# Cosformer attention feeding a low-rank mixer and an MLP: first two batches staged by halves of the heads with a direct transposed mixer output, tails padded to full 128x128 matmuls

## The chip, the cores and the metric

The kernel runs on one core of a Trainium2 chip. The metric is device time in microseconds (us) of one execution; a run is repeated and the median is taken. Names of engines as in the profile: PE (TensorE, with PEld for its weight loads), DVE (VectorE), ACT (ScalarE), POOL (GpSimd), SP (SyncE, which here only issues DMAs).

## What is computed

Eight batches, eight heads, 576 positions, head size 64. Linear attention with cosine weights comes first, then a token mixer of rank 32, then an MLP over the channels (512 to 2048 to 512):

```python
def phi(x, c, s):
    r = np.maximum(x, 0.0)
    return np.concatenate([r * c, r * s], axis=-1)
q_p = phi(q, cos_w, sin_w); k_p = phi(k, cos_w, sin_w)
kv = np.einsum('bhsf,bhsd->bhfd', k_p, v)
z = np.sum(k_p, axis=2)
num = np.einsum('bhsf,bhfd->bhsd', q_p, kv)
den = np.einsum('bhsf,bhf->bhs', q_p, z)[..., None] + 1e-06
x = num / den                       # heads side by side: (8, 576, 512)
h = x.transpose(0, 2, 1) @ U @ V
u = x + h.transpose(0, 2, 1)
out = u + np.maximum(u @ w_ch1, 0.0) @ w_ch2
```

Inputs and output are float32; the kernel computes its matmuls in bfloat16 with float32 sums.

## The kernel before

The 576 positions of a batch are four chunks of 128 and a **tail** of 64. An even batch keeps its tail in partitions 0 to 63, an odd one in 64 to 127, so that the tails of a pair of batches share one tile in the MLP. `tail(b)` is that slice of rows, and every tail operation before the MLP runs on 64 rows alone: the tail's matmuls take 64 of the array's 128 rows (or columns), and the mixer's two matmuls take 32 (`U_bf` is 128x32, `V_bf` has 32 rows).

For one batch the front part, called the mixer here, is this chain:

- loads of k, v and q (SP), `k_prep` (L184, cos and sin half of relu(k), on DVE), `q_prep` (L182, the same for q, on ACT), `v_prep` (L176, L178, casts of v on POOL into `v_ext`, whose 65th column is one, so that the sum z comes out of the same matmul);
- `kv_unit` (L219): per head five accumulating matmuls, the fifth the tail; a unit is four heads, evicted by DVE (L226);
- `qtr_unit` (L238): per chunk eight transposes of q_p on PE, evicted into `q_pT` (L111);
- `x_unit` (L254): per chunk eight matmuls that give numerator and denominator side by side, then on DVE denominator plus 1e-6 (L263), reciprocal (L266), product (L269) into `x_bf`;
- `A_unit` (L281, L288): x against U over all five chunks; `u_unit` (L298, L301): per chunk V against that, plus x, into `u_bf`; `utr_unit` (L318): four transposes per chunk of u into `uT`, which the MLP reads.

The MLP works on a pair of batches in 72 slots: sixteen `g1_main` for each batch (L332, four matmuls of 512 columns, evicted with the relu by ACT at L339), four `g1_tail` (L350) and 36 `g2_part` (L375, four matmuls each; every fourth ends in a DVE add and an output DMA, L386, L389, L393).

All order is written out by hand: each engine runs its instructions in the order of the program. First comes the mixer of batch 0 (in two halves of the heads up to x, L444 to L457), then the sixteen `g1_main(0, j)`, then the whole mixer of batch 1, then the four pairs. In a pair, `pe_plan` and `prep_plan` give the mixer's pieces of the next two batches slot numbers, and they are put between the MLP's slots. `load(b + 1)` is put eight slots after the start of batch b's plan, all three tensors at once; `k_prep` of batch 4 stands at slot 58 of pair 0, and `load(4)` at slot 55. Buffers: `kst` two, `qst` and `vst` one each, so a load waits for the preparation of the batch before.

Of the kernel before, what the change touches and what calls it, by code (L numbers as in the profile page):

```python
# [17 lines left out]
def kernel(  # L18
# [14 lines left out]
    H = 8  # L33
# [128 lines left out]
    def cast_uv():
        nc.gpsimd.tensor_copy(out=U_bf, in_=stU)
        nc.gpsimd.tensor_copy(
            out=V_bf[:, 0:4, :], in_=stV[:, 0:512].rearrange("r (p c) -> r c p", c=4)
        )
        nc.gpsimd.tensor_copy(out=V_bf[:, 4, 0:TS], in_=stV[:, 512:S])


    k_p, q_p, q_pT, kv_sb, x_bf, x_tl, A_sb = {}, {}, {}, {}, {}, {}, {}  # L170
    u_bf, u_tl, uT, uT_tl = {}, {}, {}, {}

    def v_prep(b, h0=0, h1=H):
        vx = v_ext[b % 2]
        for c in range(4):
            nc.gpsimd.tensor_copy(out=vx[:, c, h0:h1, 0:D], in_=vst[b][:, h0:h1, c, :])  # L176
        if h0 == 0:
            nc.gpsimd.tensor_copy(out=vx[tail(b), 4, :, 0:D], in_=vt[b][tail(b)])  # L178
# [9 lines left out]
    def k_prep(b, c, eng, h0=0, h1=H, half=None):  # L188
        if b not in k_p:
            k_p[b] = pool.tile([P, 5, H, 2 * D], BF16, tag="k_p", bufs=1, name="k_p")  # L190
        rows = slice(0, P) if c < 4 else tail(b)
        src = kst[b][:, h0:h1, c, :] if c < 4 else kt[b][rows, h0:h1, :]
        for i, w in enumerate((cosw, sinw)):
            if half in (None, i):
                scaled_relu(
                    eng, k_p[b][rows, c, h0:h1, i * D : i * D + D], src, w[rows, c : c + 1]
                )

    def q_prep(b, c, eng, h0=0, h1=H, half=None):
        if (b, c) not in q_p:  # L200
            q_p[b, c] = pool.tile([P, H, 2 * D], BF16, tag="q_p", bufs=5, name="q_p")
        rows = slice(0, P) if c < 4 else tail(b)
        src = qst[b][:, h0:h1, c, :] if c < 4 else qt[b][rows, h0:h1, :]
        for i, w in enumerate((cosw, sinw)):
            if half in (None, i):
                scaled_relu(
                    eng, q_p[b, c][rows, h0:h1, i * D : i * D + D], src, w[rows, c : c + 1]
                )

    def kv_unit(b, hg, tag, bufs):  # L210
# [4 lines left out]
        for i in range(4):  # L215
            h = hg * 4 + i
            for c in range(5):
                rows = slice(0, P) if c < 4 else tail(b)
                nc.tensor.matmul(  # L219
                    out=acc[:, i, :],  # L220
                    lhsT=k_p[b][rows, c, h, :],
                    rhs=vx[rows, c, h, :],
                    start=(c == 0),
                    stop=(c == 4),
                )
        nc.vector.tensor_copy(out=kv_sb[b][:, hg * 4 : hg * 4 + 4, :], in_=acc)  # L226

    def cols(c):
        return slice(c * P, c * P + P) if c < 4 else slice(512, S)

    def qtr_unit(b, c, h0=0, h1=H, eng=None):
        if b not in q_pT:
            q_pT[b] = pool.tile([P, H, S], BF16, tag="q_pT", bufs=1, name="q_pT")
        n = P if c < 4 else TS
        rows = slice(0, P) if c < 4 else tail(b)
        t_ps = ps.tile([P, H, P], BF16, tag="T", bufs=1, name="t_ps")
        for h in range(h0, h1):
            nc.tensor.transpose(  # L238
                out=t_ps[:, h, 0:n], in_=q_p[b, c][rows, h, :], identity=ident[rows, rows]
            )  # L240
        cast(eng or nc.vector, q_pT[b][:, h0:h1, cols(c)], t_ps[:, h0:h1, 0:n])

    def x_unit(b, c, hgs, tag, bufs):
        if b not in x_bf:
            x_bf[b] = pool.tile([P, 4, DM], BF16, tag="x_bf", bufs=1, name="x_bf")
            x_tl[b] = pool.tile([P, DM], BF16, tag="x_tl", bufs=1, name="x_tl")
        n = P if c < 4 else TS
        rows = slice(0, P) if c < 4 else tail(b)
        ng = len(hgs)
        acc = ps.tile([P, ng, 512], FP32, tag=tag, bufs=bufs, name="x_ps")  # L250
        for g, hg in enumerate(hgs):
            for i in range(4):
                h = hg * 4 + i
                nc.tensor.matmul(  # L254
                    out=acc[rows, g, i * E : i * E + E],
                    lhsT=q_pT[b][:, h, cols(c)],
                    rhs=kv_sb[b][:, h, :],
# [8 lines left out]
        nc.vector.reciprocal(out=rec[rows], in_=rec[rows])  # L266
        dst = x_bf[b][:, c, :] if c < 4 else x_tl[b][rows, :]
        dst = dst[:, hgs[0] * 256 : hgs[0] * 256 + ng * 256]
        nc.vector.tensor_tensor(  # L269
            out=dst.rearrange("p (g i d) -> p g i d", g=ng, d=D),  # L270
            in0=view[:, :, :, 0:D],
            in1=rec[rows].unsqueeze(3).to_broadcast([n, ng, 4, D]),
# [3 lines left out]
    def A_unit(b, tag, bufs):  # L276
        A_sb[b] = pool.tile([R, DM], BF16, tag="A_sb", bufs=2, name="A_sb")
        a_ps = ps.tile([R, DM], FP32, tag=tag, bufs=bufs, name="a_ps")
        for c in range(5):
            rows = slice(0, P) if c < 4 else tail(b)  # L280
            nc.tensor.matmul(  # L281
                out=a_ps,
                lhsT=U_bf[rows, c, :],
                rhs=x_bf[b][:, c, :] if c < 4 else x_tl[b][rows, :],
# [3 lines left out]
        nc.vector.tensor_copy(out=A_sb[b], in_=a_ps)  # L288

    def u_unit(b, c, tag, bufs):  # L290
        if b not in u_bf:
# [4 lines left out]
        n = P if c < 4 else TS  # L296
        va = ps.tile([P, DM], FP32, tag=tag, bufs=bufs, name="va_ps")
        nc.tensor.matmul(  # L298
            out=va[rows, :], lhsT=V_bf[:, c, 0:n], rhs=A_sb[b], start=True, stop=True
        )  # L300
        nc.vector.tensor_tensor(  # L301
            out=u_bf[b][:, c, :] if c < 4 else u_tl[b // 2][rows, :],
            in0=x_bf[b][:, c, :] if c < 4 else x_tl[b][rows, :],
# [3 lines left out]

    def utr_unit(b, c, eng=None):
        if b not in uT:
            uT[b] = pool.tile([P, 4, 512], BF16, tag="uT", bufs=2, name="uT")  # L310
            if b % 2 == 0:
                uT_tl[b // 2] = pool.tile([P, 4, P], BF16, tag="uT_tl", bufs=2, name="uT_tl")
        rows = slice(0, P) if c < 4 else tail(b)
        n = P if c < 4 else TS
        t_ps = ps.tile([P, H, P], BF16, tag="T", bufs=1, name="t_ps")
        for d in range(4):
            src = u_bf[b][:, c, :] if c < 4 else u_tl[b // 2][rows, :]
            nc.tensor.transpose(  # L318
                out=t_ps[:, d, 0:n], in_=src[:, d * P : d * P + P], identity=ident[rows, rows]
            )  # L320
        dst = uT[b][:, :, cols(c)] if c < 4 else uT_tl[b // 2][:, :, rows]
        cast(eng or nc.vector, dst, t_ps[:, 0:4, 0:n])
# [4 lines left out]
    def g1_main(b, j):  # L327
# [3 lines left out]
        for d in range(4):  # L331
            nc.tensor.matmul(  # L332
                out=g_ps,
                lhsT=w1_bf[:, d, j * P : j * P + P],
                rhs=uT[b][:, d, :],
# [217 lines left out]
```

## Time and profile before

| what | value |
|---|---|
| median of 3 runs | 414.84 us (414.8 to 415.09) |
| the profiled execution's own time | 414.22 us |
| its span in the trace | 412.4 us |
| PE, DVE, ACT, POOL busy | 88%, 45%, 34%, 11% of the span |
| DMA queues busy | 38% of 16 engines' span |

The span runs from the first to the last instruction, so 1.8 us of the execution's own time lie around it. A busy PE in this page is not a PE at its peak: matmuls overlap, and a matmul of 512 columns is recorded with 383 to 388 ns while the next may start after 215. The time between starts is what counts, and the chain of waits shows it, since it holds each piece only once.

### The profile page before, as it was taken

The numbers are of one execution on the slowest core, as the hardware profiler recorded it, in microseconds if no ns is written. First come the engines' busy times: TensorE is split into PE (matmuls) and PEld (weight loads), VectorE is DVE, ScalarE is ACT, GpSimd is POOL, SyncE is SP. The second block draws the span as 40 slices with busy tenths as digits, with TensorE's granted clock in tenths as the row PEclk, the third lists the DMA queues.
The fourth block names the chain that finished last, engine by engine and source line by source line (L and its number), as shares of the span: only waits on it lengthen the run. The fifth ranks groups of instructions, "written<-read, shape, count | busy, mean of one in ns | idle before, by whom it ended". The sixth has DMA issues, their size and how long they took to land.

```text
span 412.4 us, 6084 instructions
## 1 busy us (share of the span) xinstructions
PE 362.8 (88%) x2544; PEld 183.9 (45%) x2544; DVE 183.8 (45%) x408; ACT 141.4 (34%) x242; POOL 45.7 (11%) x64
## 2 busy tenths in 40 slices
PE   0546797669999994999999999999999999999996
PEld 0322245325564531465356534554475434446442
DVE  2464633564637555534355648352456552000111
ACT  1700268009462000635457005245580002664000
POOL 2453642020000001202000030020000000000000
PEclk9999998559999996999999999999999999999999
DMA  7989783920301139266000491580001121000121
GB/s 198 349 275 326 266 242 93 267 78 1 116 2 51 38 72 292 98 190 183 0 2 25 143 296 61 163 233 2 0 2 52 60 69 51 2 0 2 76 78 77
DMA packets 47533, 46.69 MB, mean 113 GB/s; under 512 B 14065, under 2 KB 38769, under 8 KB 47505
## 3 DMA queue, kind: packets, MB, share of 16 engines
q1 hardware_dynamic: 47504, 46.30, 37.5%
q8 instruction: 20, 0.33, 0.4%
q14 instruction: 9, 0.07, 0.1%
HBM read 36.86 MB, written 9.44 MB: 112 GB/s over the span
## 4 chain that ended last, share of the span: by engine, by line
PE 77%; DVE 14%; DMA 5%; issue 1%; SPq 1%; POOL 1%; DVEq 0%
PE g_ps L332 28%; PE o_ps L375 25%; PE kv_ps L219 5%; PE x_ps L254 4%; PE gt_ps L350 4%; PE va_ps L298 3%; PE t_ps L238 3%; PE t_ps L318 3%; DVE k_p L184 3%; PE a_ps L281 2%; DMA out_dram<-o_sb 2%; DVE q_pT L111 2%; DVE x_bf L269 2%; DVE u_bf L301 2%; DMA kst<-in_k_dram 2%; DMA vst<-in_v_dram 1%
## 5 line engine op out<-in xcount | busy, mean ns | idle before, releaser
L375 PE MATMUL o_ps<-w_bf,hid 128*128 128x512 bf16 x512 | 124.1, 383 | 0.0
L332 PE MATMUL g_ps<-uT,w_bf 128*128 128x512 bf16 x512 | 123.8, 388 | 0.0
L339 ACT ACTIVATE hid<-g_ps 128x512 bf16<-128x512 f32 x128 | 76.5, 597 | 130.5 <-PE g_ps L332 130.5
L332 PEld LDWEIGHTS <-w_bf 128*128 128x128 bf16 x512 | 47.5, 100 | 53.8 <-issue 7.8
L375 PEld LDWEIGHTS <-hid 128*128 128x128 bf16 x512 | 45.7, 98 | 57.5 <-issue 13.4
L386 DVE TENSOR_TENSOR o_sb<-u_bf,o_ps 128x512 f32<-128x512 bf16 x32 | 21.9, 685 | 70.0 <-PE o_ps L375 69.2
L182 ACT ACTIVATE q_p<-qst,cosw 128x512 bf16<-128x512 f32 (+1 forms) x36 | 24.0, 665 | 64.5 <-DMA qst<-in_q_dram 41.7
L176 POOL CAST v_ext<-vst 128x512 bf16<-128x512 f32 (+1 forms) x36 | 20.3, 606 | 213.3 <-DMA vst<-in_v_dram 213.3
L219 PE MATMUL kv_ps<-v_ext,k_p 128*128 128x65 bf16 (+1 forms) x320 | 26.1, 201 | 14.9 <-POOL v_ext L176 9.6
L111 DVE COPY q_pT<-t_ps 128x1024 bf16<-128x1024 bf16 (+2 forms) x45 | 26.1, 579 | 18.8 <-PE t_ps L238 18.4
L254 PE MATMUL x_ps<-kv,q_pT 128*128 128x65 bf16 (+1 forms) x320 | 19.8, 206 | 13.9 <-DVE q_pT L111 12.5
L301 DVE TENSOR_TENSOR u_bf<-x_bf,va_ps 128x512 bf16<-128x512 bf16 x32 | 21.9, 683 | 20.7 <-PE va_ps L298 20.3
L219 PEld LDWEIGHTS <-k_p 128*128 128x128 bf16 (+1 forms) x320 | 19.1, 99 | 24.1 <-DVE k_p L184 14.6
L238 PE MATMUL t_ps<-ident,q_p 128*128 128x128 bf16 (+1 forms) x320 | 26.6, 229 | 0.6 <-DVE q_pT L111 0.6
L254 PEld LDWEIGHTS <-q_pT 128*128 128x128 bf16 (+1 forms) x320 | 15.5, 107 | 25.4 <-DVE q_pT L111 15.9
L238 PEld LDWEIGHTS <-q_p 128*128 128x128 bf16 (+1 forms) x320 | 21.2, 105 | 9.4 <-issue 3.7
L298 PE MATMUL va_ps<-A_sb,V_bf 32*128 32x512 bf16 (+1 forms) x40 | 18.0, 451 | 8.1 <-DVE A_sb L288 7.0
L182 ACT ACTIVATE q_p<-qst,sinw 128x512 bf16<-128x512 f32 (+1 forms) x36 | 23.9, 664 | 0.0
L269 DVE TENSOR_TENSOR x_bf<-x_ps,rec 128x512 bf16<-128x512 f32 (+1 forms) x36 | 22.7, 632 | 1.2
L226 DVE CAST kv<-kv_ps 128x260 bf16<-128x260 f32 x16 | 6.9, 428 | 34.4 <-PE kv_ps L219 34.4
L184 DVE TENSOR_SCALAR k_p<-kst,cosw 128x512 bf16<-128x512 f32 (+1 forms) x36 | 16.1, 447 | 9.8 <-DMA kst<-in_k_dram 9.7
L184 DVE TENSOR_SCALAR k_p<-kst,sinw 128x512 bf16<-128x512 f32 (+1 forms) x36 | 20.1, 559 | 0.0
(45 smaller groups left out, 211.3 us busy)
## 6 DMA issues: line engine op xcount, KB each, us to landing
wst<-in_moe_w_ch_dram SPq DMA_DIRECT2D x8, 1024.0 KB, 6.7
out_dram<-o_sb SPq DMA_DIRECT2D x32, 256.0 KB, 2.3
kst<-in_k_dram SPq DMA_DIRECT2D x7, 1024.0 KB, 7.8
vst<-in_v_dram SPq DMA_DIRECT2D x7, 1024.0 KB, 10.6
qst<-in_q_dram SPq DMA_DIRECT2D x7, 1024.0 KB, 10.2
kt<-in_k_dram SPq DMA_DIRECT2D x8, 128.0 KB, 5.1
vt<-in_v_dram SPq DMA_DIRECT2D x8, 128.0 KB, 8.3
kst<-in_k_dram SPq DMA_DIRECT2D x2, 512.0 KB, 6.5
```

The source lines that it names most:

```text
L111: eng.tensor_copy(out=o, in_=i)
L182: nc.scalar.activation(out=o, in_=i, func=AF.Relu, bias=0.0, scale=w)
L184: eng.tensor_scalar(out=o, in0=i, scalar1=0.0, scalar2=w, op0=ALU.max, op1=ALU.mult)
L219: nc.tensor.matmul(out=acc[:, i, :], lhsT=k_p[b][rows, c, h, :], rhs=vx[rows, c, h, :], start=(c == 0), stop=(c == 4),)
L238: nc.tensor.transpose(out=t_ps[:, h, 0:n], in_=q_p[b, c][rows, h, :], identity=ident[rows, rows])
L254: nc.tensor.matmul(out=acc[rows, g, i * E : i * E + E], lhsT=q_pT[b][:, h, cols(c)], rhs=kv_sb[b][:, h, :], start=True, stop=True,)
L269: nc.vector.tensor_tensor(out=dst.rearrange("p (g i d) -> p g i d", g=ng, d=D), in0=view[:, :, :, 0:D], in1=rec[rows].unsqueeze(3).to_broa ...
L298: nc.tensor.matmul(out=va[rows, :], lhsT=V_bf[:, c, 0:n], rhs=A_sb[b], start=True, stop=True)
L301: nc.vector.tensor_tensor(out=u_bf[b][:, c, :] if c < 4 else u_tl[b // 2][rows, :], in0=x_bf[b][:, c, :] if c < 4 else x_tl[b][rows, :], i ...
L332: nc.tensor.matmul(out=g_ps, lhsT=w1_bf[:, d, j * P : j * P + P], rhs=uT[b][:, d, :], start=(d == 0), stop=(d == 3),)
L339: nc.scalar.activation(out=hid[b][:, j, :], in_=g_ps, func=AF.Relu, bias=0.0, scale=1.0)
L375: nc.tensor.matmul(out=o, lhsT=lhs[:, j, c * P : c * P + P], rhs=w2_bf[:, j, :], start=(j == 0), stop=(j == NJ - 1),)
```

## The change

**Tails.** All matmuls become 128x128. `k_tl`, `q_tl`, `q_tlT` and `x_tl` become constant tiles of 128 rows, zeroed once at the start, in which a batch writes its own half; the fifth chunk of `v_ext` is zeroed in the half that is not the batch's. `U_bf` is padded from 32 to 128 columns (with a version for each half of the tail), `V_bf` from 32 to 128 rows. The tail of u is transposed once per pair instead of once per batch.

**Batch 0.** k, q and v are prepared on both engines, the cos half on DVE, the sin half on ACT; per half of the heads come the transposes of q (evicted by ACT), `kv_unit`, `den_unit` (the denominators of all five chunks by matmuls of one column, one reciprocal for all) and five `xh_unit` of 64 columns per head. A is made in two halves of the columns. The transposed u that the MLP wants comes straight out of PE: `uTd_open` adds up x transposed (x as weights, the identity as moving operand) and `uTd_close` adds A and V. The plain u, still needed for the sum at the end, follows later between the MLP's slots.

**Batch 1.** Its mixer is put between the sixteen `g1_main(0, j)` by a table (`first`), with `uTd` for `uT` and `uTt_direct` for the pair's tail; its plain u follows in slots 17 to 21 of pair 0.

**Loads.** The tails of batch 0, U and V are issued by ACT, ahead of its first computation. k, v and q of a later batch are put one by one at 1, 3 and 12 slots after the start of the preparations. The plans of batches 2 and 3 start at slots 28 and 51 of pair 0 instead of 22 and 47.

**uT** is stored by chunk and then by channel block, so that `g1_main` reads its 512 columns as four pieces of 128.

ACT's first instructions, before (L182 is q_prep) and after (L207 is a preparation by ACT, `k_tl` the tail of k, `st_uv` the staging tile of U and V):

```order
L139 ACT_TABLE_LOAD
L139 ACTIVATE sinw<-iota 128x5
L140 ACTIVATE cosw<-iota,halfpi 128x5
L182 ACTIVATE q_p<-qt,cosw 64x4x64
L182 ACTIVATE q_p<-qt,sinw 64x4x64
```

```order
L81 DMA kt<-in_k_dram 64x8x64
L81 DMA qt<-in_q_dram 64x8x64
L81 DMA vt<-in_v_dram 64x8x64
L133 DMA st_uv<-in_moe_U_dram 128x128
L137 DMA st_uv<-in_moe_U_dram 64x32 x2
L138 DMA st_uv<-in_moe_V_dram 32x576
L155 ACT_TABLE_LOAD
L155 ACTIVATE sinw<-iota 128x5
L156 ACTIVATE cosw<-iota,halfpi 128x5
L207 ACTIVATE k_tl<-kt,sinw 64x4x64
```

Seven DMA issues now stand ahead of the table load and of the two weights that every preparation reads.

ACT around the first sixteen `g1_main`, before (L339 evicts them, L182 prepares batch 1) and after (L475 evicts them, L207 prepares batch 1):

```order
L109 ACTIVATE uT_tl<-t_ps 128x4x64
L339 ACTIVATE hid<-g_ps 128x512 x16
L182 ACTIVATE q_p<-qst,cosw 128x8x64
L182 ACTIVATE q_p<-qst,sinw 128x8x64
L182 ACTIVATE q_p<-qst,cosw 128x8x64
```

```order
L475 ACTIVATE hid<-g_ps 128x512
L207 ACTIVATE k_tl<-kt,sinw 64x8x64
L207 ACTIVATE k_p<-kst,sinw 128x8x64
L475 ACTIVATE hid<-g_ps 128x512
L207 ACTIVATE k_p<-kst,sinw 128x8x64 x2
L475 ACTIVATE hid<-g_ps 128x512
L207 ACTIVATE k_p<-kst,sinw 128x8x64
L475 ACTIVATE hid<-g_ps 128x512 x2
```

What stood as one block of sixteen evictions followed by batch 1 now alternates.

SP in pair 0, before and after, where k of batch 4 is loaded (`kst_1532` before, `kst_1299` after; the other rows store finished chunks, the one of 64 rows the tails):

```order
L393 DMA out_0_dram<-o_sb_1332 128x512
L393 DMA out_0_dram<-o_sb_1449 128x512
L389 DMA out_0_dram<-o_sb_1528 64x512 x2
L77 DMA kt_1535<-in_k_dram 64x8x64
L71 DMA kst_1532<-in_k_dram 128x8x256
L77 DMA vt_1536<-in_v_dram 64x8x64
```

```order
L529 DMA out_0_dram<-o_sb_1250 128x512
L529 DMA out_0_dram<-o_sb_1291 128x512
L81 DMA kt_1300<-in_k_dram 64x8x64
L75 DMA kst_1299<-in_k_dram 128x8x256
L81 DMA vt_1329<-in_v_dram 64x8x64
```

The load of k moved ahead of the third, fourth and fifth chunk's stores.

The diff, cut to what the text speaks of:

```diff
-    load_tail(kt[0], k, 0)
-    load_tail(vt[0], v, 0)
+    load_tail(kt[0], k, 0, A_)
+    load_tail(qt[0], q, 0, A_)
+    load_tail(vt[0], v, 0, A_)
     for h0 in (0, 4):
         load_main(kst[0], k, 0, h0, h0 + 4)
+        load_main(qst[0], q, 0, h0, h0 + 4)
         load_main(vst[0], v, 0, h0, h0 + 4)
...
+    U_bf = const.tile([P, 6, P], BF16)
+    V_bf = const.tile([P, 5, P], BF16)
...
     def kv_unit(b, hg, tag, bufs, eng=None):
...
             for c in range(5):
-                rows = slice(0, P) if c < 4 else tail(b)
                 nc.tensor.matmul(
                     out=acc[:, i, :],
-                    lhsT=k_p[b][rows, c, h, :],
-                    rhs=vx[rows, c, h, :],
+                    lhsT=k_p[b][:, c, h, :] if c < 4 else k_tl[:, h, :],
+                    rhs=vx[:, c, h, :],
...
+    def den_unit(b, hg, tag, bufs):
+        d_ps = ps.tile([P, 5, 4], FP32, tag=tag, bufs=bufs, name="d_ps")
+        for c in range(5):
+            for i in range(4):
+                h = hg * 4 + i
+                nc.tensor.matmul(
+                    out=d_ps[:, c, i : i + 1],
+                    lhsT=qT_of(b, c, h),
+                    rhs=kv_sb[b][:, h, D:E],
...
+    def uTd_open(b, d, tag, bufs):
...
+        for c in range(4):
+            nc.tensor.matmul(
+                out=t[:, c, :], lhsT=x_bf[b][:, c, d * P : d * P + P], rhs=ident,
+                start=(c == 0), stop=False,
+            )
+    def uTd_close(b, d, eng):
...
+            out=t.rearrange("m c t -> m (c t)"), lhsT=A_sb[b][:, d * P : d * P + P],
+            rhs=V_bf[:, 0:4, :].rearrange("r c t -> r (c t)"), start=False, stop=True,
...
     def g1_main(b, j):
...
-                out=g_ps,
+                out=g_ps.rearrange("p (c t) -> p c t", c=4),
                 lhsT=w1_bf[:, d, j * P : j * P + P],
-                rhs=uT[b][:, d, :],
+                rhs=uT[b][:, :, d, :],
...
+    for c in ORD:
+        k_prep(0, c, (V_, A_), 0, 4)
+    for c in ORD:
+        q_prep(0, c, (V_, A_), 0, 4)
+    cast_uv()
+    v_prep(0, 0, 4, ORD)
+    for c in ORD:
+        qtr_unit(0, c, 0, 4, A_, "g", 3)
+    kv_unit(0, 0, "T", 1)
+    for c in ORD:
+        k_prep(0, c, (V_, A_), 4, 8)
+    rec0 = den_unit(0, 0, "X", 1)
...
+    for c in ORD:
+        xh_unit(0, c, 1, rec1, "o", 2)
+    for d in range(2):
+        uTd_open(0, d, "g", 3)
+        uTd_close(0, d, A_)
...
+    for n, c in enumerate(ORD):
+        at(n // 2, lambda c=c: k_prep(1, c, (V_, A_)))
+        at(4 + n // 2, lambda c=c: q_prep(1, c, (V_, A_)))
+    for n, c in enumerate(ORD):
+        at(1 + n // 2, lambda c=c: u_unit(0, c, "o", 2))
...
+    at(7, lambda: kv_unit(1, 0, "o", 2), lambda: kv_unit(1, 1, "o", 2))
+    for n, c in enumerate(ORD):
+        at((7, 7, 8, 9, 10)[n], lambda c=c: x_unit(1, c, "X", 1))
+    at(11, lambda: A_unit(1, "o", 2))
+    for d in range(4):
+        at(11 + d // 2, lambda d=d: uTd_open(1, d, "o", 2), lambda d=d: uTd_close(1, d, V_))
+    at(13, lambda: uTt_direct(0, "T", 1, V_))
     for j in range(NJ):
         g1_main(0, j)
+        for t in first.get(j, []):
+            t()
...
+        def put_loads(at, b):
+            for n, t in zip((1, 3, 12), loads(b)):
+                put(at + n, t)
...
-                    if b + 1 < B:
-                        put(w + 8, lambda b=b: load(b + 1))
+                    if b + 1 < B:
+                        put_loads(w - (9 if pr == 0 else 6), b + 1)
```

More of the change, by code (lines that the diff above doesn't have):

```diff
@@ L162, in cast_uv @@
[L162 to L170, printed above, removed]
+    q_tl = const.tile([P, H, 2 * D], BF16)
+    q_tlT = const.tile([P, H, P], BF16)
+    x_tl = const.tile([P, DM], BF16)
+    U_bf = const.tile([P, 6, P], BF16)
@@ L287, in A_unit @@
             )
-        nc.vector.tensor_copy(out=A_sb[b], in_=a_ps)
+        cast(eng or V_, A_sb[b][:, n0:n1], a_ps[:, n0:n1])
+        return a_ps
     def u_unit(b, c, tag, bufs):
```

419 lines of the change are left out of this document (269 added, 150 removed).

## The prediction, as it was put on record

> **What bounds the kernel now.** I read the stages first (busy time by windows cut where the chain of waits changes its work): staging of batch 0, the first sixteen `g1_main`, the mixer of batch 1, the rest of pair 0, pair 1.
>
> ```profile
> 0.00:48.16 48.16, 21.25 (x151) 11.36 (x152) 23.36 (x73) 12.37 (x27) 18.89 (x32) 1.00 0.91 281
> 48.16:64.46 16.30, 16.30 (x68) 6.99 (x68) 6.75 (x9) 9.34 (x16) 7.95 (x3) 1.00 0.91 268
> 64.46:91.13 26.67, 16.89 (x151) 9.69 (x148) 14.79 (x32) 6.81 (x11) 5.75 (x10) 0.60 0.50 137
> 91.13:175.41 84.28, 75.86 (x572) 38.44 (x573) 47.06 (x105) 29.93 (x50) 4.16 (x5) 0.94 0.28 82
> 175.41:261.02 85.61, 85.06 (x637) 43.65 (x636) 44.43 (x95) 33.83 (x56) 6.01 (x10) 1.00 0.39 112
> ```
>
> The columns are the window, its length, then busy time of PE, PEld, DVE, ACT, POOL, the granted clock, DMA share and GB/s. From 91 us on PE is busy nearly throughout: there only PE's own work counts, and PE's waits. Before that PE idles for more than half of the staging and a third of batch 1's mixer, each a serial chain through PE and DVE. Next I read that chain in order of time (start, length, what), first the end of batch 0's staging, then a piece of batch 1's mixer:
>
> ```profile
> 35.56 2.37 PE a_ps L281 x5
> 37.95 0.69 DVE A_sb L288
> 38.68 0.59 PE va_ps L298
> 39.30 0.70 DVE u_bf L301
> 40.05 0.61 PE t_ps L318 x4
> ...
> 48.16 16.30 PE g_ps L332 x64
> ...
> 68.57 0.44 PE x_ps L254 x8
> ...
> 69.24 0.21 DVE rec L266
> 69.48 0.69 DVE x_bf L269
> ```
>
> Each link waits for the one before; nothing of the MLP fills the holes, because PE's order has none there. A third reading is the timeline of pair 0, around the only long hole behind 91 us:
>
> ```profile
> 159.10 0.48 DVE L184 TENSOR_SCALAR k_p<-kst,cosw 128x512 bf16<-128x512 f32 x1 [7.02 <-DMA kst<-in_k_dram]
> 160.62 0.67 DVE L288 CAST A_sb<-a_ps 32x512 bf16<-32x512 f32 x1
> 161.35 0.58 PE L298 MATMUL va_ps<-A_sb,V_bf 32*128 32x512 bf16 x1 [5.48 <-DVE A_sb L288]
> 161.86 1.89 PE L375 MATMUL o_ps<-w_bf,hid 128*128 128x512 bf16 x4
> ...
> 165.97 1.03 PE L375 MATMUL o_ps<-w_bf,hid 128*128 128x512 bf16 x4
> ```
>
> DVE waits 7.02 us for k of batch 4, A's eviction stands behind that on DVE, and PE behind A. Four matmuls then take 1.89 us instead of 1.03: the clock had dropped.
>
> **Tails.** The chain in pair 0 prices a matmul of partial shape:
>
> ```profile
> 99.11 0.86 PE g_ps L332 x4
> ...
> 100.50 1.34 PE kv_ps L219 x20
> 101.84 0.97 PE g_ps L332 x4
> ...
> 105.12 0.45 PE t_ps L238 x8
> ...
> 105.56 0.26 PE x_ps L254 x8
> ...
> 108.00 0.39 PE t_ps L238 x8
> ...
> 114.66 0.38 PE x_ps L254 x8
> ...
> 116.93 1.28 PE a_ps L281 x5
> ...
> 120.08 0.32 PE va_ps L298
> ```
>
> Matmuls of 65 columns cost 0.26/8 = 0.033 us in `x_unit`, but 1.34/20 = 0.067 in `kv_unit`, where every fifth is of 64 rows. A matmul of 512 columns costs 0.86/4 = 0.215; `va_ps` (32 rows) takes 0.32, and the four of the MLP behind a partial one 0.97 instead of 0.86. So each change of shape costs about 0.1 us, and with all matmuls 128x128 there is none. Per batch: kv 2 x (1.34 - 0.67) = 1.3; five `u_unit` 5 x (0.32 - 0.215 + 0.11) = 1.1; A 1.28 - 1.08 + 0.11 = 0.3; the tail in `x_unit` 0.38 - 0.26 + 0.11 = 0.2; q's tail transposes 0.39 + 0.11 - 0.45, nearly nothing, since they become wider; one instead of two tail transposes of u per pair, about 0.25 a batch. Sum 3.2, for batches 2 to 7, whose mixers lie where PE is the bound: 19. Some falls where PE waits for DVE anyway, so I take **-18**; ends 0 and -20. DVE and ACT, next late there, have 44 and 34 busy of 85.6 us and leave room.
>
> The Trainium skill ("TensorE: Matmul & The Clock Gate", section "Why this matters for your kernels") says that a matmul of 32 rows alone takes the same time as one of 128. By that padding would be worth nothing and the sum end 18 higher; the 0.067 against 0.033 above speaks against reading it so for mixed shapes.
>
> **The hole in pair 0.** `load(4)` moves from slot 55 to slots 43, 45 and 54, ahead of three stores, with `k_prep` still at 58. Fifteen slots of at least 0.86 us are 13 us and more, against the 7 us by which k came late, so the hole goes: 5.5, and the slow clock behind it, eight MLP matmuls and two `va_ps`, some 1.8. **-7.3**. What is late next there is DVE: the plans of batches 2 and 3 start later (28 and 51), and are as dense. Batch 1's five `u_unit` are added to these slots, 5 x 0.215 = **+1.1**. For new waits for DVE I allow **+2.5** (0 to 6; 6 is what would put the hole back in another place).
>
> **Staging of batch 0.** The steps are priced from these rows of the first 23 us, and one of the DMA issues (median us to landing at the end):
>
> ```profile
> 0.73 1.28 ACT L139 ACT_TABLE_LOAD   x1 [0.73 <-PEq L537]
> 2.22 0.62 SPq L71 DMA_DIRECT2D kst<-in_k_dram  x1
> 7.14 0.35 DVE L184 TENSOR_SCALAR k_p<-kst,cosw 128x256 bf16<-128x256 f32 x1 [2.72 <-DMA kst<-in_k_dram]
> 7.41 0.35 DVE L184 TENSOR_SCALAR k_p<-kst,sinw 128x256 bf16<-128x256 f32 x1
> 12.14 0.49 ACT L182 ACTIVATE q_p<-qst,cosw 128x256 bf16<-128x256 f32 x1
> 12.54 0.49 ACT L182 ACTIVATE q_p<-qst,sinw 128x256 bf16<-128x256 f32 x1
> 17.19 1.08 POOL L164 CAST V_bf<-stV 32x512 bf16<-32x512 f32 x1
> 18.40 1.43 POOL L176 CAST v_ext<-vst 128x256 bf16<-128x256 f32 x4
> 22.05 2.08 POOL L111 CAST w_bf<-wst 128x2048 bf16<-128x2048 f32 x1 [0.39 <-DMA wst<-in_moe_w_ch_dram]
> 22.26 2.01 DVE L184 TENSOR_SCALAR k_p<-kst,sinw 128x256 bf16<-128x256 f32 x1
> ...
> stV<-in_moe_V_dram SPq DMA_DIRECT2D x1, 72.0 KB, 5.7
> ```
>
> ACT now issues seven DMAs first, 0.62 each. The sixth reuses the semaphore of k's first half, so it waits until that has landed: 7.14 - 2.22 = 4.9 after its issue, now 0.73 + 4.9 = 5.6. Two more issues: 6.9. Table load and both weights, 1.28 + 0.5: 8.7, when before they were there at 2.4. So this move costs the preparations 8.7 - 7.1 = 1.6. ACT: ten halves at 0.40 to 12.7, five evictions of q at about 0.5 to 15.2. POOL: V lands at 6.3 + 5.7 = 12.0; the casts of U and V, about 2.2, to 14.2; those of v, 1.43 + 0.4, to 16.0; then three heads of `kv_unit`, PE at half clock: 17.3. From there one chain: kv's eviction 0.43; denominators 1.3 beside k's second half on DVE, 5 x 0.26 = 1.3, held up by POOL's first cast of w1 as in the row at 22.26 (2.01 for 0.35), +1.9; reciprocals 0.7; q's second half 1.3; transposes and five products 2.6: 25.6. Then kv, its eviction, denominators, reciprocals 3.3; first half of A 1.3; five products 2.0; `uTd_open` 0.4; second half of A 1.3, evicted 0.4; close and eviction 1.2: 35.6. Some 25 hand-overs of 0.05 make **37** (34, without the cast's hold and with the q's evictions hidden, to 41, if the loads come 4 later) instead of 48.16: **-11.2**. What goes is mostly the row from 38.7 to 48.2, five chunks one after the other.
>
> **First sixteen g1_main with batch 1.** PE's own work at full clock: 64 x 0.215 = 13.8; kv 40 x 0.033 = 1.3; transposes 40 x 0.056 = 2.2; x 1.3; A 1.1; batch 0's `u_unit` 1.1; four `uTd` 4 x (0.22 + 0.215) = 1.7; the tail about 0.6. Together 23. The clock starts low, as in the row at 48.16 (16.30 for 64 x 0.215 = 13.8): +2.5. DVE has about 18 to 20 us here, ACT 17 (sixteen evictions, ten halves, three of q's evictions); PE's order waits for DVE at the `u_unit` beside `k_prep`, and five times for a chunk of x (0.44 + 0.21 + 0.69 and hand-overs, 1.6, of which one `g1_main` covers 0.86): 3.7. POOL's casts of w1 and w2 hold DVE up to 1.9 each, six of them, of which I count two: 3.8. Sum **33**, between 25.5 (no wait) and 43, today's 16.30 + 26.67: **-10**.
>
> **Sum.** -11.2 - 10 + 1.1 - 7.3 + 2.5 - 18 = -42.9. Against the profiled execution's own 414.2 (span 412.4 and 1.8 around it) that is 371.3; its median is 0.6 higher, so I say **372**. Pair 3's own part has no mixer and stays.
>
> **Rivals.**
> 1. *Padding gives nothing*: the 0.1 us belongs to the tails' extra waits, not to the shape. Against it, `va_ps` pays it with no new wait. 372 + 18 = 390. Chance 0.10.
> 2. *The first mixers stay serial*: DVE, held by POOL's casts, bounds the interleaved stretch, and it takes 43 as today. For it: DVE's 20 us and six casts in one stretch. 382. Chance 0.13.
> 3. *The split moving operand is slow*: `g1_main` now reads four pieces of 128. No row shows such a read. Priced as four matmuls of 128 columns it is 4 x 0.056 = 0.224, +0.009 each, 512 of them, +4.6; priced at nothing it is 0, which I take. It decides if a matmul costs over 0.215 + 42.9/512 = 0.30 us: then the kernel is slower than before, and at 0.32 it ends at 372 + 54 = 426. Chance 0.03.
> 4. *The change does not reach the end*: the stages shift but PE's waits return in pair 0 and 1 as they leave the start, by DVE, and all that is left is half the padding and the hole: 414.8 - 16 = 399. Chance 0.04.
>
> My forecast has 0.70. Its own bounds: low, staging 3 and the stretch 4 less, no new waits 2.5: 363. High: staging 41, new waits 6, split reads 4.6: about 385, which takes rival 2 in. So 363 to 387; outside lie rivals 1, 3 and 4, with 0.17. A measurement of this kernel tells about 0.2% (0.8 us) from no change. Faster 0.95: the forecast and rivals 1, 2 and most of 4; same 0.01; slower 0.04, rival 3 and a hole as in pair 0 that none of this sees.
>
> **What would show it.** In the profile after: `kv_ps` x20 in about 0.67 and `va_ps` in 0.22 in the chain; the first g_ps at about 37 and the seventeenth near 70 us; no DVE wait for `kst` in pair 0; a pair's length of 79 to 80 us instead of 85.6; g_ps still 0.86 for four. A pair still 85 long says rival 1, a seventeenth g_ps at 80 rival 2, four g_ps over 1.2 us rival 3.

## The result and the profile after

The changed kernel takes **376.16 us** (median of 4 runs, 374.04 to 377.03) against 414.86 before: ratio 0.9059, 95% interval 0.9019 to 0.9098. The profiled execution took 376.63 us, 374.5 of them span.

The stages of the changed kernel, cut at the same places as before (first and seventeenth `g1_main`, pairs 1, 2 and 3); columns as in the prediction:

```profile
0.00:38.17 38.17, 17.10 (x190) 13.89 (x191) 16.29 (x53) 15.87 (x36) 14.78 (x35) 1.00 1.00 288
38.17:73.16 34.99, 28.09 (x228) 14.55 (x227) 23.51 (x41) 17.85 (x29) 14.27 (x11) 0.90 0.97 284
73.16:147.92 74.76, 68.36 (x575) 37.49 (x573) 49.94 (x108) 30.40 (x51) 9.42 (x15) 1.00 0.49 138
147.92:228.32 80.40, 78.41 (x636) 43.54 (x634) 43.85 (x94) 34.28 (x56) 4.61 (x9) 1.00 0.40 115
228.32:308.08 79.76, 78.24 (x633) 43.55 (x632) 40.45 (x84) 27.94 (x46) 1.44 (x3) 1.00 0.14 44
308.08:374.50 66.42, 62.45 (x337) 30.08 (x335) 6.87 (x10) 21.51 (x36) 0.00 (x0) 1.00 0.11 40
```

Every stage with a mixer is shorter, by 10.0, 8.0, 9.5, 5.2 and 5.3 us; the last, without one, is what it was. In pair 1 PE's busy time fell from 85.06 to 78.41 at the same number of instructions, so the gain there is in the matmuls themselves. The chain of waits after (start, length, what) shows which:

```profile
75.05 0.22 PE va_ps L383
75.26 0.86 PE g_ps L468 x4
...
88.77 0.61 PE kv_ps L241 x20
```

`va_ps` went from 0.32 to 0.22, `kv_ps` from 1.34 to 0.61, and the four matmuls of the MLP behind them from 0.97 to 0.86. The same 0.86 shows that reading the moving operand in four pieces costs nothing.

The staging did not become as short as forecast. The timeline of its start, on ACT and POOL:

```profile
6.57 1.15 ACTq L137 DMA_DIRECT2D st_uv<-in_moe_U_dram  x2
9.99 0.34 ACTq L138 DMA_DIRECT2D st_uv<-in_moe_V_dram  x1
10.37 1.28 ACT L155 ACT_TABLE_LOAD   x1 [10.37 <-DMA qt<-in_q_dram]
...
11.77 0.28 ACT L156 ACTIVATE cosw<-iota,halfpi 128x5 f32<-128x5 f32 x1
...
14.88 1.10 POOL L185 CAST V_bf<-st_uv 32x512 bf16<-32x512 f32 x1 [1.01 <-DMA st_uv<-in_moe_V_dram]
...
16.64 1.43 POOL L199 CAST v_ext<-vst 128x256 bf16<-128x256 f32 x4
```

Two of the seven issues on ACT were held: the fifth, the first of two of U's tail, until k's tail had landed (issued at 0.74, 5.8 us to landing), the seventh, V, until q's tail had (issued at 1.50, 8.5 to landing). The weights of all preparations stand behind them: ready at 12.05 us. V itself landed only 4.8 us after its issue, at 14.8, and on POOL v's casts stand behind those of U and V, until 18.07. The same timeline in the first `g1_main`, where DVE is held:

```profile
37.99 1.89 POOL L115 CAST w_bf<-wst 128x2048 bf16<-128x2048 f32 x1 [0.36 <-DMA wst<-in_moe_w_ch_dram]
38.88 1.28 DVE L209 TENSOR_SCALAR k_tl<-kt,cosw 64x512 bf16<-64x512 f32 x1
40.18 2.92 DVE L209 TENSOR_SCALAR k_p<-kst,cosw 128x512 bf16<-128x512 f32 x3
40.70 2.11 POOL L115 CAST w_bf<-wst 128x2048 bf16<-128x2048 f32 x1 [0.81 <-DMA wst<-in_moe_w_ch_dram]
43.02 0.67 DVE L384 TENSOR_TENSOR u_tl<-x_tl,va_ps 64x512 bf16<-64x512 bf16 x1
43.73 0.38 PE L383 MATMUL va_ps<-A_sb,V_bf 128*128 128x512 bf16 x1 [2.08 <-DVE u_tl L384]
44.21 0.47 DVE L209 TENSOR_SCALAR k_p<-kst,cosw 128x512 bf16<-128x512 f32 x1
```

A preparation takes 0.47 without such a neighbour (last row). The one at 38.88 took 1.28 and ends 0.28 behind POOL's first cast of w1; of the three at 40.18 the last, which starts at 40.98, took 2.12 and ends 0.28 behind the second cast. So each of the two was held until the cast beside it had ended. u of batch 0 stands behind them on DVE, and PE, whose third `va_ps` needs a free buffer, waits 2.08. That pause is followed by a slow clock (granted clock 0.53, the third figure from the end):

```profile
44.80:48.20 3.40, 3.40 (x10) 1.24 (x9) 2.33 (x5) 0.60 (x1) 2.18 (x2) 0.53 0.70 270
```

### The profile page after: what moved, and what is told of

It reads as the page before. It is cut to its first block, busy times and chain, and to the rows that moved or that the text cites. A ratio compares the mean times of both kernels' runs of the same rounds, so it can differ in the third digit from the quotient of the medians.

```text
span 374.5 us, 6199 instructions
## 1 busy us (share of the span) xinstructions
PE 332.6 (89%) x2589; PEld 183.1 (49%) x2589; DVE 180.9 (48%) x389; ACT 147.9 (39%) x254; POOL 44.5 (12%) x70
## 4 chain that ended last, share of the span: by engine, by line
PE 73%; DVE 14%; ACT 5%; issue 3%; DMA 3%; POOL 1%; ACTq 1%; POOLq 0%; DVEq 0%
PE o_ps L511 27%; PE g_ps L468 26%; PE t_ps L258 4%; DVE k_p L209 4%; PE kv_ps L241 3%; PE gt_ps L486 3%; DMA st_uv<-in_moe_U_dram 3%; PE x_ps L340 3%; PE a_ps L366 2%; ACT q_p L207 2%; PE va_ps L383 2%; DVE o_sb L522 2%; DVE u_bf L384 1%; PE t_ps L409 1%; DVE x_bf L350 1%
## 5 line engine op out<-in xcount | busy, mean ns | idle before, releaser
L475 ACT ACTIVATE hid<-g_ps 128x512 bf16<-128x512 f32 x128 | 76.3, 596 | 128.6 <-PE g_ps L468 128.6
L115 DVE COPY q_pT<-t_ps 128x1024 bf16<-128x1024 bf16 x26 | 17.9, 689 | 20.4 <-PE t_ps L258 20.4
L258 PE MATMUL t_ps<-ident,q_p 128*128 128x128 bf16 x256 | 21.0, 230 | 3.9 <-ACT q_p L207 3.3
L258 PEld LDWEIGHTS <-q_p 128*128 128x128 bf16 x256 | 17.7, 103 | 11.5 <-ACT q_p L207 5.6
L207 ACT ACTIVATE q_p<-qst,sinw 128x512 bf16<-128x512 f32 (+1 forms) x36 | 23.2, 662 | 0.0
L350 DVE TENSOR_TENSOR x_bf<-x_ps,rec 128x512 bf16<-128x512 f32 x28 | 19.4, 691 | 1.0
L383 PE MATMUL va_ps<-A_sb,V_bf 128*128 128x512 bf16 x40 | 15.2, 384 | 4.5 <-DVE u_bf L384 2.3
L207 ACT ACTIVATE q_p<-qst,cosw 128x512 bf16<-128x512 f32 x24 | 17.0, 710 | 1.5 <-DMA qst<-in_q_dram 1.4
L207 ACT ACTIVATE q_tl<-qt,cosw 64x512 bf16<-64x512 f32 x6 | 4.3, 717 | 32.7 <-PE t_ps L258 22.1
L115 POOL CAST w_bf<-wst 128x2048 bf16<-128x2048 f32 x8 | 15.5, 1934 | 14.4 <-DMA wst<-in_moe_w_ch_dram 14.4
L292 DVE TENSOR_SCALAR rec<-x_ps 128x8 f32<-128x8 f32 (+1 forms) x35 | 5.8, 165 | 20.9 <-PE x_ps L340 20.7
L340 PEld LDWEIGHTS <-q_pT 128*128 128x128 bf16 x224 | 10.5, 100 | 10.2 <-DVE x_bf L350 4.0
L486 PE MATMUL gt_ps<-uT_tl,w_bf 128*128 128x128 bf16 x256 | 15.4, 219 | 0.0
```

The costliest lines, as they stand in the source:

```text
L115: eng.tensor_copy(out=o, in_=i)
L207: nc.scalar.activation(out=o, in_=i, func=AF.Relu, bias=0.0, scale=w)
L258: nc.tensor.transpose(out=t_ps[:, h, :], in_=q_p[b][:, c, h, :] if c < 4 else q_tl[:, h, :], identity=ident,)
L350: nc.vector.tensor_tensor(out=x_of(b, c, rows).rearrange("p (g i d) -> p g i d", g=2, d=D), in0=view[:, :, :, 0:D], in1=rec[rows].unsqueez ...
L383: nc.tensor.matmul(out=va, lhsT=V_bf[:, c, :], rhs=A_sb[b], start=True, stop=True)
L475: nc.scalar.activation(out=hid[b][:, j, :], in_=g_ps, func=AF.Relu, bias=0.0, scale=1.0)
```

## The experiments

My theory: three separate causes. Padding saves a change of matmul shape at every tail and every rank-32 matmul, the split loads take away the hole in pair 0, and batches 0 and 1 gain by a shorter chain and by interleaving. The rivals were that padding saves nothing, and that the interleaving does not matter. Executions of the changed kernel scatter by 1.5 us either way, so smaller differences between medians say nothing. The stages say more, except the stretch of the first `g1_main` with batch 1: in two runs with the same code there it took 34.99 and 32.76.

**Padding alone**, on the kernel before (`k_tl`, `q_tl`, `q_tlT`, `x_tl` as zeroed constants, U and V padded, the pair's tail of u transposed once):

```diff
-                    lhsT=k_p[b][rows, c, h, :],
-                    rhs=vx[rows, c, h, :],
+                    lhsT=k_p[b][:, c, h, :] if c < 4 else k_tl[:, h, :],
+                    rhs=vx[:, c, h, :],
```

> The kernel before with the padding alone: every matmul 128x128, the pair's tail of u transposed once; staging, order, slots, loads and the layout of uT as before. Theory (each change of matmul shape costs PE about 0.1 us, and padding takes them away): 3.2 us a batch for batches 2 to 7, and a part of it for batches 0 and 1, whose mixers are a chain through PE: 414.9 - 18 to - 22, so 393 to 397, with kv_ps x20 at about 0.65 us in the chain and pairs of about 80 us. Rival 1 (the 0.1 us belongs to the waits of the tails): 413 to 415, pairs of 85.6. If nearly all of the 38.7 us that the change saves were padding, it would be under 385.

Measured: 394.68 us (394.33 to 395.42), ratio 0.9521 (0.9499 to 0.9542): 19.8 us, as the theory says. Its timeline still has the hole:

```profile
151.70 0.48 DVE L198 TENSOR_SCALAR k_p<-kst,cosw 128x512 bf16<-128x512 f32 x1 [7.45 <-DMA kst<-in_k_dram]
```

**U and V alone padded**, on the kernel before (the tails stay at 64 rows):

```diff
-    U_bf = const.tile([P, 5, R], BF16)
-    V_bf = const.tile([R, 5, P], BF16)
+    U_bf = const.tile([P, 5, P], BF16)
+    V_bf = const.tile([P, 5, P], BF16)
```

> The kernel before with only U and V padded from a rank of 32 to 128; the tails stay at 64 rows. It tells the shape of 32 rows (mixer) from that of 64 (tails). Theory: per batch four of the five u_unit lose 0.32 - 0.215 + 0.11 = 0.21 us each, A one change of shape, 0.1; the tails' changes stay: 0.95 us a batch, over eight batches 6 to 8: 407 to 409. Rival (a matmul of 32 rows costs what one of 128 does, so that only the 64-row tails pay): 414 to 415.

Measured: 412.2 us (410.74 to 412.3), ratio 0.9933 (0.9907 to 0.9959). Only 2.3 us, nearer to the rival. Its pairs 1 and 2:

```profile
175.42:260.97 85.55, 82.88 (x627) 44.55 (x636) 44.80 (x95) 33.82 (x56) 6.12 (x10) 1.00 0.40 112
260.97:344.12 83.15, 82.47 (x626) 44.55 (x636) 40.59 (x85) 27.59 (x46) 2.90 (x5) 1.00 0.24 72
```

Pair 2 lost 1.9 us as forecast (two batches, 0.95 each), pair 1 nothing: 85.55 against 85.61. In pair 1 DVE waits for a store that stands among the loads, first in this kernel, then in the one before:

```profile
247.97 0.69 DVE L389 TENSOR_TENSOR o_sb<-u_bf,o_ps 128x512 f32<-128x512 bf16 x1 [1.41 <-DMA out_dram<-o_sb]
```

```profile
248.03 0.69 DVE L386 TENSOR_TENSOR o_sb<-u_bf,o_ps 128x512 f32<-128x512 bf16 x1 [0.68 <-DMA out_dram<-o_sb]
```

Both start pair 1 at 175.4 and leave this wait at the same time, though ahead of it A's eviction came 1.0 us earlier with the padding (242.33 instead of 243.36): what PE saved ahead of the wait was only waited longer. In pair 0 the hole for k does the same: from the first `g1_main` to pair 1 it is 127.6 us against 127.3. A gain that lies ahead of a wait with a fixed end is not seen.

**Loads alone**, on the kernel before (`put_loads` in place of `load`; the two loads of a pair's plans):

```diff
-                        put(w + 8, lambda b=b: load(b + 1))
+                        put_loads(w - (9 if pr == 0 else 6), b + 1)
...
-                put(71, lambda nb=nb: load(nb + 3))
+                put_loads(58, nb + 3)
```

> The kernel before with only the loads moved: k, v and q of a later batch one by one, at 1, 3 and 12 slots after the start of the preparations, the plans' starts as before (22 and 47 in pair 0). Theory: the 7.02 us wait of DVE for k of batch 4 goes, with it 5.5 us of PE and the slow clock behind it: 414.9 - 7 = 408 (407 to 410). Rival (the hole only moves, DVE or the queues are late next): 413 to 415. Pairs 1 and 2 stay at 85.6 either way.

Measured: 407.29 us (407.05 to 407.64), ratio 0.9825 (0.98 to 0.9849): 7.2 us, the hole and no more: 6.6 of it lie in the rest of pair 0 (77.69 instead of 84.28).

**Padding and loads together:**

> The kernel before with the padding and the split loads together, staging and batch 1's serial mixer as before. Alone they took 19.8 and 7.2 us. Theory (they act in different places and add up; the padded kernel still has the hole in pair 0, of 6.72 us and 1.90 behind it): 414.5 - 27 = 387.5, 386 to 389. What is then left to the changed kernel, some 11 us, is the work on batches 0 and 1. Rival (the wait for k only turns into the next wait, for stores or for DVE, once PE is faster): 391 or more.

Measured: 384.63 us (384.22 to 385.25), ratio 0.9262 (0.9234 to 0.9291): 30.6 us below its 415.28 of before, 3.7 more than the sum of the two and below the range of the theory. With the loads spread, the waits with a fixed end no longer eat what padding saves: alone it took 3.0 off the rest of pair 0 (81.25) and 4.8 off pair 1 (80.86); on top of the spread loads it takes 5.5 (77.69 to 72.20) and 6.3 (85.03 to 78.73). Its rest of pair 0, pairs 1 and 2:

```profile
87.35:159.55 72.20, 68.14 (x570) 37.44 (x569) 46.64 (x104) 29.80 (x50) 5.09 (x9) 0.98 0.46 130
159.55:238.28 78.73, 78.24 (x634) 43.58 (x633) 43.97 (x94) 33.84 (x56) 4.48 (x9) 1.00 0.42 121
238.28:316.36 78.08, 78.08 (x634) 43.58 (x633) 40.47 (x84) 27.60 (x46) 1.94 (x4) 1.00 0.14 45
```

All three are shorter than in the changed kernel (74.76, 80.40, 79.76): that one gives back 2.6 + 1.7 + 1.7 us.

**Where pairs 1 and 2 give it back.** In the changed kernel PE waits 1.5 us for ACT in each (1.49 and 1.52), as the timeline of pair 1 shows:

```profile
186.82 0.72 ACT L207 ACTIVATE q_tl<-qt,cosw 64x512 bf16<-64x512 f32 x1
...
188.16 0.72 ACT L207 ACTIVATE q_tl<-qt,sinw 64x512 bf16<-64x512 f32 x1
188.90 0.72 ACT L207 ACTIVATE q_p<-qst,cosw 128x512 bf16<-128x512 f32 x1
189.53 0.70 ACT L207 ACTIVATE q_p<-qst,sinw 128x512 bf16<-128x512 f32 x1
...
190.28 0.62 PE L258 MATMUL t_ps<-ident,q_p 128*128 128x128 bf16 x8 [1.49 <-ACT q_p L207]
```

`prep_plan` now prepares q's tail first, `pe_plan` still transposes chunk 0 first. One line undoes it:

```diff
+        for n, c in enumerate(range(5)):
             for i in range(2):
                 engs = (A_, None) if i == 0 else (None, A_)
```

> The changed kernel with one line different: in the plan of the preparations q's chunks are prepared in the order in which they are transposed (0, 1, 2, 3, tail) instead of tail first. Theory (the waits of 1.87 us at 188.41 and 1.90 us at 268.81 come from this order: chunk 0 of q is transposed at slot 37 and its second half is prepared at that very slot): both go, 376.2 - 3.5 = 372.7 (372 to 373.5). Rival (ACT is late there whatever the order, because of its evictions): 375.5 to 376.5.

Measured: 370.64 us (369.06 to 372.95), ratio 0.8929 (0.8885 to 0.8972). Its windows:

```profile
144.47:223.21 78.74, 78.24 (x636) 43.57 (x633) 43.89 (x94) 33.83 (x56) 4.37 (x9) 1.00 0.39 116
223.21:301.28 78.07, 78.07 (x633) 43.60 (x632) 40.47 (x84) 27.60 (x46) 2.18 (x4) 1.00 0.14 45
```

The pairs are 1.7 us shorter each and equal to those of padding and loads alone, so the theory holds there. The median is 1.4 below its range; in the profiled executions 2.2 us more lie in the stretch with batch 1 (32.76 against 34.99), which the edit does not touch: the scatter named above. PE's wait for u is 1.27 there instead of 2.08, and the clock stays at 1.00 behind it.

**The change of shape, taken apart.** First the tails of `kv_unit` at 64 rows again, in the changed kernel, in the old order; then the same matmuls with a unit's four tails behind each other:

```diff
-                    lhsT=k_p[b][:, c, h, :] if c < 4 else k_tl[:, h, :],
-                    rhs=vx[:, c, h, :],
+                    lhsT=k_p[b][:, c, h, :] if c < 4 else k_tl[tail(b), h, :],
+                    rhs=vx[:, c, h, :] if c < 4 else vx[tail(b), c, h, :],
```

> The changed kernel with one step of the padding undone: the fifth matmul of every head in kv_unit runs on the 64 rows of the tail again, the order as it is (per head four full chunks, then the tail). Theory (each change of matmul shape costs PE about 0.1 us; there are eight in a unit and sixteen units): kv_ps x20 at 1.34 us instead of 0.61, 376.2 + 16 x 0.73 = 388, 385 to 388 since a part falls into waits. Rival (partial rows cost nothing in themselves): 376.

Measured: 389.12 us (386.92 to 389.64), ratio 0.9376 (0.9346 to 0.9406). The chain:

```profile
91.54 1.34 PE kv_ps L241 x20
92.88 0.97 PE g_ps L468 x4
```

```diff
-        for i in range(4):
-            h = hg * 4 + i
-            for c in range(5):
+        for c in range(5):
+            for i in range(4):
+                h = hg * 4 + i
...
-                    start=(c == 0),
-                    stop=(c == 4),
+                    start=(c == 0 and i == 0),
+                    stop=(c == 4 and i == 3),
```

> The same matmuls as in the kernel with 64-row tails in kv_unit, in another order: for each chunk the four heads, so that a unit's four tail matmuls follow each other at its end. It tells the change of shape from the shape itself. Theory (the change costs): two changes a unit instead of eight, kv_ps x20 at 0.8 to 0.85 us, 376.2 + 16 x 0.2 = 379.5 (378 to 381). Rival (a matmul of 64 rows is itself slow, 0.15 us each more): as much as with the tails between, 385 to 388.

Measured: 379.44 us (377.57 to 380.77), ratio 0.915 (0.9115 to 0.9185). The chain:

```profile
86.76 0.74 PE kv_ps L241 x20
87.50 0.97 PE g_ps L468 x4
```

In both the last change of a unit falls to the matmuls of the MLP behind it, 0.97 instead of 0.86. So the same four 64-row matmuls cost 0.73 + 0.11 = 0.84 us a unit between full ones, with eight changes, and 0.13 + 0.11 = 0.24 behind each other, with two (the length of pair 1, which holds four units, says 0.24 as well: 81.36 against 80.40). The difference of six changes gives 0.10 us each, and 0.24 - 2 x 0.10 leaves 0.01 for each 64-row matmul: it is the change that costs, and not the 64 rows.

**U and V at rank 32 again**, in the changed kernel:

```diff
-    U_bf = const.tile([P, 6, P], BF16)
-    V_bf = const.tile([P, 5, P], BF16)
+    U_bf = const.tile([P, 6, R], BF16)
+    V_bf = const.tile([R, 5, P], BF16)
```

> The changed kernel with U and V at their rank of 32 again: A_unit's matmuls take 32 columns, va_ps and uTd_close 32 rows. Theory (a change of shape costs 0.1 us, where no other wait hides it): per batch five va_ps and one A_unit with two changes each, 1.2 us, 376.2 + 8 x 1.2 = 386 (382 to 386). Rival (32 rows are nearly free, as the padding of U and V alone made the kernel before only 2.3 us shorter): 377 to 379.

Measured: 384.63 us (382.66 to 386.03), ratio 0.9275 (0.9235 to 0.9315): 8.5 us, where padding U and V in the kernel before gave 2.3. The chain has both prices, that of the small matmul and that of the full ones behind it:

```profile
78.91 0.32 PE va_ps L383
79.22 0.97 PE g_ps L468 x4
```

**Batch 1's mixer behind the `g1_main`** instead of between them, in the changed kernel (its transposes, kv, x, A, uTd):

```diff
-    at(11, lambda: A_unit(1, "o", 2))
+    late.append(lambda: A_unit(1, "o", 2))
```

> The changed kernel with batch 1's mixer (transposes, kv, x, A, uTd) taken out from between the sixteen g1_main and put behind them in one piece; the preparations and batch 0's u_unit stay between them, uTd and the padding stay. Theory (the interleaving is what shortened this stretch): the loop takes 18 to 20 us and the mixer alone 20 or more, 40 to 43 instead of 35: 376 + 5 to 8, so 381 to 384. Rival (uTd and the preparations shared by two engines did it, the interleaving adds little, since DVE bounds the stretch either way): 376 to 379.

Measured: 379.36 us (378.44 to 380.4), ratio 0.915 (0.9124 to 0.9175): 3.2 us more. In its profiled execution the stretch is 4.8 longer than the 34.99 of the changed kernel:

```profile
37.49:77.33 39.84, 28.86 (x226) 15.12 (x226) 23.12 (x40) 18.44 (x30) 15.69 (x14) 0.87 0.88 270
```

That lies between theory and rival. Even serial, the stretch is 3.1 us shorter than the 42.97 of before, and padding and loads alone brought it to 40.68. So of its 8 us the interleaving gives 3.2 to 4.8, the rest padding and the shorter chain. The 2.2 by which this stretch scatters blurs that split: against the 32.76 it would be 7.1.

**Batch 0 without the direct transposed output:** A whole, then chunk by chunk `u_unit`, transposes, eviction.

```diff
-    for d in range(2):
-        uTd_open(0, d, "g", 3)
-        uTd_close(0, d, A_)
-    uTd_open(0, 2, "g", 3)
     A_unit(0, "X", 1, V_, 256, 512, a0)
-    uTd_open(0, 3, "o", 2)
-    uTd_close(0, 2, V_)
-    uTd_close(0, 3, A_)
+    for c in range(4):
+        u_unit(0, c, "o", 2) if c % 2 else u_unit(0, c, "g", 3)
+        utr_unit(0, c, A_)
```

> The changed kernel with the four chunks of batch 0 brought to uT the way of before: A whole, then per chunk u_unit on PE and DVE, four transposes and an eviction by ACT, one chunk after another; no uTd for batch 0, and its u_unit leave the first g1_main. Theory (the direct transposed output is what shortens the end of the staging, where before took 1.9 us a chunk): first g1_main at 43 instead of 38.2, the stretch behind it 1 to 2 shorter: 379 to 381. Rival (the chunks overlap, and the direct output gains nothing): 375 to 377.

Measured: 379.32 us (377.83 to 379.5), ratio 0.9126 (0.9098 to 0.9153). Staging and stretch:

```profile
0.00:44.25 44.25, 18.62 (x190) 13.51 (x191) 20.34 (x58) 17.06 (x38) 18.63 (x36) 1.00 0.94 267
44.25:76.35 32.10, 26.33 (x223) 14.32 (x222) 18.25 (x35) 17.14 (x28) 10.68 (x9) 0.95 1.00 303
```

The start is 6.1 us later. The stretch, which four `u_unit` left, is 2.9 shorter; how much of that is its scatter is open. By the medians the direct output is worth 3.2 us, a part of it paid back by making u later.

**U and V later**, in the changed kernel: issued by SP behind batch 0's loads, cast behind both halves of v.

```diff
-    A_.dma_start(out=stV, in_=moe_V)
+    nc.sync.dma_start(out=stV, in_=moe_V)
...
-    cast_uv()
     v_prep(0, 0, 4, ORD)
...
     v_prep(0, 4, 8, ORD)
+    cast_uv()
```

> The changed kernel with U and V issued by SP behind batch 0's six loads instead of by ACT ahead of its table load, and their casts on POOL behind both halves of v. ACT then issues three DMAs before its first computation. Theory (the weights at 12.05 us and v's casts behind those of U and V hold the staging; A needs U only at 30 us): weights at about 4.7, first kv_unit done some 3 to 4 us earlier, first g1_main at 34 to 35 instead of 38.2: 372 to 373. Rival (k, q and v land no earlier, and v's landing at 10.65 and 12.30 us sets the start anyway): 375 to 376.5.

Measured: 368.73 us (368.36 to 370.45), ratio 0.8887 (0.8857 to 0.8916). Its windows and its timeline:

```profile
0.00:33.83 33.83, 16.56 (x191) 13.44 (x192) 16.10 (x53) 16.09 (x36) 12.71 (x30) 1.00 1.04 271
33.83:65.23 31.40, 26.71 (x228) 14.20 (x227) 21.78 (x41) 17.63 (x29) 14.35 (x10) 0.95 0.91 295
```

```profile
4.27 0.28 ACT L156 ACTIVATE cosw<-iota,halfpi 128x5 f32<-128x5 f32 x1
...
12.80 0.39 POOL L201 CAST v_ext<-vt 64x256 bf16<-64x256 f32 x1 [9.69 <-DMA vt<-in_v_dram]
```

The weights are there at 4.55 instead of 12.05, and v's casts now wait for v alone: the first `g1_main` is 4.3 us earlier, a little more than forecast. The two halves of the edit, issues and casts, were not tried apart. The median is 3 us below the range of the theory, since the stretch became 3.6 shorter too: PE's wait of 2.08 for u is gone and the granted clock is 0.95 instead of 0.90. That this comes from the edit is not shown; the stretch was 2.2 shorter in a run that left it alone.

**Both edits, and other starts in pair 0:**

```diff
-                starts = (28, 51, 24)
+                starts = (22, 46, 28)
```

> The changed kernel with three edits: U and V issued by SP behind batch 0's loads, with their casts behind v's; q's chunks prepared in the order in which they are transposed; the plans of batches 2 and 3 in pair 0 start at slots 22 and 46 instead of 28 and 51 and are spread by 28/36 instead of 24/36, which puts more MLP slots between the x_unit that wait for each other. Theory: the first gives 7.4 and the second 3.4 in places that don't meet, 365.3; the third takes part of the 6 us of holes above 0.7 us in pair 0, 1 to 4: 361 to 364.5. Rival (with earlier plans in pair 0 k of batches 3 and 4 is late again, as in the kernel before): 367 to 372, with a DVE wait for kst of several us in pair 0.

Measured: **362.71 us** (362.26 to 365.55), ratio 0.8772 (0.8734 to 0.8811), the fastest of all. From the start to pair 2:

```profile
0.00:34.30 34.30, 17.50 (x190) 13.83 (x191) 16.08 (x53) 16.09 (x36) 12.87 (x30) 1.00 1.04 281
34.30:66.06 31.76, 25.42 (x228) 13.50 (x227) 23.45 (x44) 17.80 (x29) 14.36 (x10) 1.00 0.89 273
66.06:136.68 70.62, 66.67 (x575) 37.78 (x574) 49.41 (x106) 30.16 (x51) 10.24 (x16) 1.00 0.62 179
136.68:215.60 78.92, 78.40 (x636) 43.56 (x634) 44.42 (x95) 33.82 (x56) 5.56 (x11) 1.00 0.42 120
```

The rest of pair 0 went from 74.76 to 70.62, DVE waits for no load of k there, and the granted clock reads 1.00 in all four rows.

## Why the prediction was right, step by step

| stage (us, profiled) | before | padding and loads | changed kernel |
|---|---|---|---|
| staging | 48.1 | 46.7 | 38.2 |
| first `g1_main`, batch 1 | 43.0 | 40.7 | 35.0 |
| rest of pair 0 | 84.3 | 72.2 | 74.8 |
| pair 1 | 85.6 | 78.7 | 80.4 |
| pair 2 | 85.0 | 78.1 | 79.8 |
| pair 3 and end | 66.4 | 66.4 | 66.4 |

- *Padding, -18*: right in mechanism and size. 19.8 alone; with the loads spread too, pairs 1 and 2 are 6.9 shorter each, where 3.2 a batch gives 6.4. What I had not seen: part of it only shows once no wait with a fixed end follows.
- *Rival 1, padding gives nothing*: fell. The Trainium skill ("TensorE: Matmul & The Clock Gate", section "Why this matters for your kernels"), from which it came, speaks of one matmul of 32 rows; the run with the tails grouped fits it for 64 rows (0.74 for twenty), and the run with them between full ones (1.34) shows that the price is at the changes. That a change of tiling mode drains TensorE is a rule of the Trainium skill too ("TensorEngine Tiling (Array Packing)", section "Key Properties"); it gives no figure; these runs fit it, at 0.10 us a change.
- *The hole, -7.3*: 7.2 alone.
- *Staging, 37*: 38.17. The step that failed is the weights at 8.7: I let ACT's sixth issue wait for k's first half, but the fifth waited for k's tail and the seventh for q's, and they came at 12.05; V, for which I had 12.0, was there at 14.8. With v's casts done at 18.07 instead of 16.0 this cost 1.9 at the end of the first kv; the chain behind it took 18.9 us where I had 19.7. Moving U and V gave 4.3.
- *The stretch, 33*: 34.99. Mis-sized were two terms. With PE's own work at the 23 of the sum and the slow clock at 3.4 at most (two windows of 3.4 us at about half, 0.53 and 0.52), PE's waits are 8.6 or more, where I had 7.5; the longest, at 43.73, is 2.08. That the 2.5 for the clock came near is luck: I put it at the start, as in the kernel before, where twelve matmuls fill 48.16 to 52.88, 0.39 us each (the column of the clock reads 1.00 there, so it does not show this slow start). In the changed kernel eight `g1_main` matmuls take the 2.02 us from 38.17 on, 0.25 each; the two slow windows came later. Rival 2 was partly right: serial costs 3.2 to 4.8 (7.1 against the shorter run), not 10, since padding and the direct output shorten the serial mixer as well.
- *New waits, +2.5 for DVE*: they came to 4.9, and most of it is ACT's. Pairs 1 and 2 lost 3.4 to ACT, by the order of q, which the prediction leaves out; pair 0 lost 2.6 against padding and loads alone, of which batch 1's `u_unit` are 1.1 by the estimate of the prediction, and the rest is DVE's, for which PE waits 5.9 us there instead of 3.9.
- *Rival 3, the split read*: four matmuls still take 0.86. *Rival 4*: fell with the pairs at 80.

Forecast -42.9, measured 414.22 - 376.63 = 37.6 between the profiled executions. The shortfall is 1.2 in the staging, 2.0 in the stretch, 1.7 in the pairs, and 0.3 around the span.

## What to carry to other kernels

Count the changes of matmul shape, not the idle rows: pad, or put the odd shapes behind each other. Before an edit's worth is summed, look for the next wait whose end something else fixes (a load, a store); an edit ahead of it is worth nothing until that wait is gone, and both together give more than their sum. When one list of work is reordered, reorder the lists that consume it, and keep DMA issues that nobody needs early off an engine that computes first.

## What the runs showed of the hardware

- Matmuls of 65 columns on 64 rows are not slow in `kv_unit` (0.01 us more than full ones), only the changes between them and full ones: 0.10 us each, and the full ones behind a partial one pay too (0.97 instead of 0.86 for four).
- A slow clock can follow a short pause of PE: in the changed kernel two windows of about 3.4 us at half clock (0.53 and 0.52) stand in the stretch with batch 1, the first behind the pause of 2.08. In the fastest kernel the pause there is 0.85, no such window follows, and the stretch is 31.76 instead of 34.99. The length of the pause alone does not settle it: with the tails grouped it was 2.33, and the clock stayed at 1.00 behind it. How much of the difference is the clock was not tried by itself.
